# Routed two-layer network on one core: blocks of 512 rows with seven products, convolution in channel units over whole sequences

## The chip, the cores and the metric

The kernel runs on one NeuronCore of a Trainium2 chip. Its engines work side by side, each through its own instructions in order: TensorE (PE, with its weight loads as PEld), VectorE (DVE), ScalarE (ACT), GpSimd (POOL) and SyncE (SP), which here only issues transfers. The metric is the device time of one execution in microseconds (us). Before the change the median of three runs is 1327.32 us (1325.98 to 1328.85).

## The reference

The input is 8 sequences of 3584 tokens with 192 channels. First a causal convolution of 7 taps runs along each sequence; its taps are a softmax of `weight`, one set for each of 8 heads of 24 channels. Then each token is sent to one of 8 experts:

```python
out = np.einsum('hk,bskhg->bshg', w, x_unf)            # the convolution
logits = np.einsum('bsd,de->bse', x, w_gate)
local_gate = 1.0 / (1.0 + np.exp(-np.einsum('bsd,de->bse', x, w_local).squeeze(-1)))
e = fresh_e if s == 0 or local_gate[b, s] < 0.5 else prev_e
h = np.maximum(x[b, s] @ w1[e], 0.0)                   # 192 -> 1024
out[b, s] = p[e] * (h @ w2[e])                         # 1024 -> 192
```

A token whose local gate is at least one half keeps the expert of the token before it, so the choice runs along the sequence. `p` is the softmax of the logits. All values are 32-bit floats.

## The kernel before

**Groups and units.** The 28672 tokens are cut into 16 groups of 1792 (`PT`), two to a sequence. A unit is 128 rows of one expert (`UT`). Once a group is routed, its rows are scattered into a table in DRAM (`slots`), where each expert has its own stretch; units are read back from there.

**Groups 0 and 1** go a short way of their own at the start: `wide` (L195) does the convolution and the logits with TensorE, `wide_route` (L393) the routing. **Groups 2 to 15** are convolved by `conv` (L366): for each head ACT multiplies by the first tap (L377, 128x336) and DVE adds six more taps (L387). `route` (L601) then makes logits (`logits`, L565: DVE transposes into `z`, TensorE multiplies at L580, ACT copies to `ls`), carries the choice along the sequence with scans, and appends the rows to `to_put`. `table` (L788) writes which expert and which row of `slots` each coming block has.

**Blocks.** A block is one or two units of one expert (`n` = 1 or 2; `KT` = 2 is the most). The list (L885) has 35 blocks of one unit, then 87 of two, then 20 of one; two more single units stand behind a branch at the end (`spare`, L1108 and L1155) that is taken only when the table has something for them. How many blocks are surely full after each group is worked out ahead by `_sure` (L48) from the worst case, so the list does not depend on the data; which expert a block has is read from the table when it runs.

**One block** is: `load_w` (L897), 1536 KB of the expert's weights into one of four buffers `wb`; `load_rows` (L907), its rows into one of six buffers `xg`; `turn` (L928), transposes on TensorE into PSUM (`xps`) and four ACT copies to `xT`; `hidden` (L952), the first layer, 24 matmuls of 64 rows of the array times 128 columns for `n` = 2, in two PSUM pairs, each ended by two ReLU evictions on ACT (L968); `output` (L973), the second layer, 32 matmuls for `n` = 2, ended for each unit by an ACT eviction with scale (L988), a DVE addition (L992) and an indirect DMA of POOL that scatters the rows to the output (L996). A matmul uses half of the array's rows (`halves`), two run at once, and the profile has two records for each.

**The order of work** is written out by hand. In the loop over blocks (L1138) come the rows three blocks ahead (`ensure`, L1090), the weights three blocks ahead (`weights`, L1101), `hidden` of this block, `turn` of the next, `output` of this one. At three places of each block `step(time)` (L1037) inserts convolution or routing work for DVE until the given budget is used up; each piece of that work carries its own cost as a number (`yield 0.6`). `put` (L768) inserts one scatter of 128 rows into `slots` on POOL, behind a given instruction. Since every engine takes its instructions in order, this order decides what waits behind what. SP issues rows and then weights, and a load of convolution input from within `conv` (L385).

Of the kernel before, what the change touches and what calls it, by code (L numbers as in the profile page):

```python
# [9 lines left out]
I32 = mybir.dt.int32  # L10
# [23 lines left out]
NX = NT + HALO  # L34
# [4 lines left out]
KT = BT // P  # L39
# [4 lines left out]
EARLY = 3  # L44
SPARE = 2

# [5 lines left out]


ONE = [_sure(min(g + 1, EARLY) * PT, UT) for g in range(NPART)]
TWO = [_sure((g + 1) * PT - ONE[-1] * UT, BT) if g >= EARLY else 0 for g in range(NPART)]
# [3 lines left out]
FULL = {0: ONE[0], HALF: _sure(PT + PT // 2, UT), **{g: ONE[g] for g in range(1, NPART)}}  # L59
REST = NU - ONE[-1] - 2 * TWO[-1]  # L60
# [21 lines left out]
def kernel(  # L82
# [13 lines left out]
    xs = ctx.enter_context(tc.tile_pool(name="xs", bufs=2))  # L96
    ys = ctx.enter_context(tc.tile_pool(name="ys", bufs=4))
# [3 lines left out]
    xp = ctx.enter_context(tc.tile_pool(name="xp", bufs=6))  # L101
    tp = ctx.enter_context(tc.tile_pool(name="tp", bufs=1))
    hp = ctx.enter_context(tc.tile_pool(name="hp", bufs=1))
    op = ctx.enter_context(tc.tile_pool(name="op", bufs=2))
    xps_p = ctx.enter_context(tc.tile_pool(name="xps_p", bufs=1, space=PSUM))
    hps_p = ctx.enter_context(tc.tile_pool(name="hps_p", bufs=4, space=PSUM))
    yps_p = ctx.enter_context(tc.tile_pool(name="yps_p", bufs=2, space=PSUM))
# [6 lines left out]
    def load_x(g):  # L114
        x_sb = xs.tile([P, NX, D], F32, name="x_sb")
        src = x[g // PER]
        win = bass.AP(tensor=src.tensor, offset=src.offset + g % PER * PT * D,
                      ap=[[NT * D, P], [1, NX * D]])
        nc.sync.dma_start(out=x_sb.rearrange("p t d -> p (t d)"), in_=win)
        return x_sb  # L120

    def load_b(g):

        x_sb = xs.tile([P, NX, D], F32, name="x_sb")
        xv = x_sb.rearrange("p t d -> p (t d)")[:, :NB * D].rearrange("p (b d) -> p b d", d=D)
# [12 lines left out]
    with tc.tile_pool(name="scr", bufs=1) as scr:  # L138
# [4 lines left out]
        x_in = {0: load_b(0)}  # L143
        wg = cst.tile([P, 3 + DQ, Q], F32, name="wg")
        nc.sync.dma_start(out=wg, in_=wgl)
        x_in[1] = load_b(1)
# [43 lines left out]
    def z_tile():  # L190
        return yt.tile([P, 3 * NH * TB + NB * DR], F32, name="z")
# [3 lines left out]
    def wide(g, xv, y_sb, both):  # L195
# [58 lines left out]
        yr = zy[:TB, 3 * NH * TB:].rearrange("p (b d) -> p b d", d=DR)  # L254
# [17 lines left out]
        lt = sm.tile([P, NB, E + 1], F32, name="lt")[:TB]  # L272
# [9 lines left out]
    pi = cst.tile([P, 2], I32, name="pi")  # L282
    nc.gpsimd.iota(pi, pattern=[[0, 2]], base=0, channel_multiplier=1)
    ti0 = cst.tile([P, NT], I32, name="ti0")
# [78 lines left out]
    def row_tile():  # L363
        return ys.tile([P, NB, DG], F32, name="y_sb")
# [869 lines left out]
```

## Time and profile before

| what | value |
|---|---|
| median of three runs | 1327.32 us |
| the profiled execution | 1326.81 us |
| its span, first to last instruction | 1325.1 us |
| PE busy | 1304.4 us (98%) |
| DVE, ACT, POOL busy | 778.3, 625.2, 480.4 us |
| mean granted TensorE clock | 0.998 |
| moved by DMA | 325.29 MB, mean 245 GB/s |

The span is cut into 40 slices of 33 us in the page's second part, and each digit there is a busy share in tenths. A line of a group gives the source line, engine, operation, tiles written and read, shapes and count; then the busy time of the group and the mean duration of one in nanoseconds; then the idle time of the engine just before them and what ended it. In the timeline a line gives start and length of a run of like instructions and their count. PE's records overlap, so their starts tell more than their lengths.

### The profile page before, as it was taken

How to read it: one execution, taken by the hardware profiler on the slowest of the kernel's cores; microseconds unless marked ns; L12 is line 12 of the kernel's file. 1: busy time of each engine (PE TensorE's matmuls, PEld its weight loads, DVE VectorE, ACT ScalarE, POOL GpSimd, SP SyncE). 2: the span in 40 equal slices, each digit the busy share in tenths (PEclk: the TensorE clock that was granted, in tenths of full speed). 3: DMA queues.
4: the chain of work that ended last, by engine and by line, in shares of the span. 5: the costliest groups of instructions: out<-in, count | busy, mean ns of one | idle time of the engine just before them, and what ended most of it. 6: DMA issues, size and time to landing. Idle time of an engine off the chain costs nothing. (4 is left out here: it accounts for less than half of the span.)

```text
span 1325.1 us, 41356 instructions
## 1 busy us (share of the span) xinstructions
PE 1304.4 (98%) x16682; PEld 1260.9 (95%) x16682; DVE 778.3 (59%) x2434; ACT 625.2 (47%) x1571; POOL 480.4 (36%) x520
## 2 busy tenths in 40 slices
PE   9899999999999999999999999999999999999997
PEld 7799999999999999999999999999999999999997
DVE  6888898977878787878777878785610000000000
ACT  5345555544454545444545454544444444444553
POOL 4445352534343434343434343434344212211111
PEclk9999999999999999999999999999999999999999
DMA  5789999967575757575757575756565555556893
GB/s 188 283 349 391 376 365 345 394 213 266 182 275 177 290 188 277 201 260 192 271 186 273 193 271 199 267 195 210 197 211 205 189 185 188 192 187 229 313 317 131
DMA packets 67298, 325.29 MB, mean 245 GB/s; under 512 B 12576, under 2 KB 38103, under 8 KB 47650
## 3 DMA queue, kind: packets, MB, share of 16 engines
q1 hardware_dynamic: 44784, 277.41, 58.4%
q0 software_dynamic: 22320, 45.22, 9.2%
q8 instruction: 133, 2.18, 0.7%
q14 instruction: 59, 0.48, 0.1%
q10 hardware_dynamic: 2, 0.00, 0.0%
HBM read 277.29 MB, written 45.77 MB: 244 GB/s over the span
## 5 line engine op out<-in xcount | busy, mean ns | idle before, releaser
L980 PE MATMUL yps<-wb,hT 64*128 64x192 f32 x7328 | 641.0, 325 | 5.8 <-ACT hT L968 2.8
L963 PE MATMUL hps<-xT,wb 64*128 64x256 f32 (+1 forms) x6816 | 637.2, 336 | 1.7 <-issue 1.4
L963 PEld LDWEIGHTS hps<-xT,wb 64*128 64x128 f32 x6816 | 589.1, 187 | 27.2 <-issue 4.0
L980 PEld LDWEIGHTS yps<-wb,hT 64*128 64x128 f32 x7328 | 602.8, 187 | 11.1 <-issue 4.6
L996 POOL DMA_INDIRECT out_dram<-o_sb,xg x229 | 232.3, 1014 | 605.7 <-DVE o_sb L992 533.9
L968 ACT ACTIVATE hT<-hps 128x512 f32<-128x512 f32 (+1 forms) x568 | 261.9, 512 | 361.4 <-PE hps L963 246.5
L387 DVE SCALAR_TENSOR_TENSOR y_sb<-x_sb,c,y_sb 128x336 f32<-128x336 f32 x672 | 376.5, 570 | 18.9 <-issue 0.8
L992 DVE SCALAR_TENSOR_TENSOR o_sb<-yps,xg,o_sb 128x192 f32<-128x192 f32 x229 | 87.5, 414 | 467.8 <-ACT o_sb L988 461.4
L775 POOL DMA_INDIRECT slots<-y_sb,posi x228 | 231.2, 1014 | 209.3 <-ACT xT L949 114.8
L988 ACT ACTIVATE o_sb<-yps,xg 128x192 f32<-128x192 f32 x229 | 86.9, 418 | 289.8 <-PE yps L980 287.4
L949 ACT COPY xT<-xps 64x256 f32<-64x256 f32 (+4 forms) x568 | 210.8, 371 | 11.7 <-issue 1.7
L377 ACT ACTIVATE y_sb<-x_sb,c 128x336 f32<-128x336 f32 x112 | 63.7, 581 | 0.0
L359 PEld LDWEIGHTS xps<-ident,xg 64*128 64x128 f32 (+1 forms) x916 | 57.0, 124 | 5.2
L359 PE MATMUL xps<-ident,xg 64*128 64x64 f32 (+1 forms) x916 | 60.0, 217 | 0.0
L570 DVE STREAM_TRANSPOSE z<-y_sb 128x768 f32<-128x768 f32 (+1 forms) x56 | 45.4, 853 | 0.4
L596 DVE COPY lt<-lq 32x36 f32<-32x36 f32 x224 | 40.8, 182 | 3.5
L580 PE MATMUL hps<-z,wg 64*32 64x128 f32 x1344 | 24.2, 272 | 1.2 <-issue 1.2
L580 PEld LDWEIGHTS hps<-z,wg 64*32 64x32 f32 x1344 | 19.2, 105 | 4.1 <-issue 2.9
L556 PE MATMUL yps<-y_sb,hot 112*128 112x194 f32 x64 | 12.6, 353 | 1.4 <-DVE hot L550 1.1
L556 PEld LDWEIGHTS yps<-y_sb,hot 112*128 112x128 f32 x64 | 11.3, 202 | 2.1 <-DVE hot L550 1.6
L672 DVE COPY bk<-so_far 1x32 f32<-1x32 f32 x56 | 12.3, 220 | 0.7
L588 DVE STREAM_TRANSPOSE lq<-ls 128x256 f32<-128x256 f32 x14 | 6.2, 441 | 10.9 <-ACT ls L585 10.9
(236 smaller groups left out, 358.0 us busy)
## 6 DMA issues: line engine op xcount, KB each, us to landing
wb<-in_w_dram SPq DMA_DIRECT2D x138, 1536.0 KB
x_sb<-in_x_dram SPq DMA_DIRECT2D x14, 1920.0 KB
xg<-slots SPq DMA_DIRECT2D x87, 195.0 KB
wb<-in_w_dram SPq DMA_DIRECT2D x12, 512.0 KB
xg<-slots SPq DMA_DIRECT2D x53, 97.5 KB
out_dram<-o_sb,xg POOLq DMA_INDIRECT x229
slots<-y_sb,posi POOLq DMA_INDIRECT x228
x_sb<-in_xb_dram SPq DMA_DIRECT2D x4, 768.0 KB
```

Source lines behind the costliest of these rows:

```text
L359: nc.tensor.transpose(to, src[rows], identity=ident[rows, rows])
L377: nc.scalar.activation(cols(h), chans(h, 0), Act.Copy, scale=c[:, h, 0:1])
L387: nc.vector.scalar_tensor_tensor(cols(h), chans(h, k), c[:, h, k:k + 1], cols(h), Alu.mult, Alu.add)
L570: nc.vector.transpose(z[:, t:u, :], y_sb[:, t:u, Y0:Y0 + D])
L775: ins = nc.gpsimd.indirect_dma_start(out=slots[:, :], in_=rows, in_offset=None, out_offset=bass.IndirectOffsetOnAxis(ap=to, axis=0)).ins
L949: copied = nc.scalar.copy(a, b)
L963: nc.tensor.matmul(hps[half][:, j, w], lhsT=wb[rows, f0:f0 + P], rhs=xT[rows, d, w], start=(d == 0 and j == 0), stop=(d == KD - 1), skip_g ...
L968: relu = nc.scalar.activation(hT[:, m:m + 2, w], hps[half][:, :, w], Act.Relu)
L980: nc.tensor.matmul(yps[half][:, k * D:(k + 1) * D], lhsT=hT[rows, m, k * P:(k + 1) * P], rhs=wb[rows, WA + m * D:WA + (m + 1) * D], start= ...
L988: nc.scalar.activation(o_sb[:, k, :], y[k][0], Act.Copy, scale=xg[:, k, 0:1])
L992: nc.vector.scalar_tensor_tensor(o_sb[:, k, :], y[k][1], xg[:, k, 0:1], o_sb[:, k, :], Alu.mult, Alu.add)
L996: sent = nc.gpsimd.indirect_dma_start(out=out, in_=o_sb[:, k, :], in_offset=None, out_offset=bass.IndirectOffsetOnAxis(ap=xg.bitcast(I32)[ ...
```

## The change

- **Blocks of four units.** `KT` is now 4. The list becomes 51 blocks of one unit, 20 of two, 31 of four, none of a further kind of two, and 14 of one; behind the branch stand 28 single units, the first two in one branch and the rest in a second one inside it. Besides `_sure` there is `_likely`, which counts blocks as full that the worst case would not fill; `LOSE` units are held in reserve for it. The last single units form a group of their own (`PADS`), which waits for the filler rows; the others no longer do.
- **Seven products.** For a block of four units, the first layer's 192 input channels are three depths of 64 in each half of the array. For the first two depths, two row halves (256 rows) and two column halves of the weights are a 2x2 by 2x2 product of pieces, done with seven products in place of eight (`seven`), with sums of rows (`combine_x`, five DVE operations) and of weights (`combine_w`, four POOL operations on 256 columns, one in place). The third depth keeps four products. Partial sums are kept by ACT copies and joined by three DVE additions; ReLU follows. `output` then runs in two parts.
- **PSUM.** After the start, four pools of one pair of banks each (`xps_p`, `wps_p`, `yps_p`, `zps_p`) serve all uses.
- **Convolution.** The input is laid out by head. A unit of work is one head (24 channels) of one group (groups 2 and 3) or of a double group of 3584 rows, a whole sequence (the other twelve groups as six). `tap` starts a unit, `taps` may start some ahead. `route`, `logits` and their tiles take 28 rows per partition for a double group. The logits' matmuls are placed by `visit` in the middle of a later block's output or by the next step, in two halves.
- **Order.** SP issues tokens (`tokens`, at most two units of input per block), then weights, then rows. `step` carries an overshoot over to the next one; the budgets change.

The core of the diff:

```diff
-    xs = ctx.enter_context(tc.tile_pool(name="xs", bufs=2))
-    ys = ctx.enter_context(tc.tile_pool(name="ys", bufs=4))
+    xs = ctx.enter_context(tc.tile_pool(name="xs", bufs=1))
+    ys = ctx.enter_context(tc.tile_pool(name="ys", bufs=3))
...
+ONE = {g: _sure((g + 1) * PT, UT) if g + 1 < EARLY else _likely(EARLY * PT, UT, LEFT1) for g in GROUPS}
...
+blocks += [(2, 4, i, next(g for g in GROUPS if i < FOUR[g])) for i in range(FOUR[LAST])]
+blocks += [(3, 2, i, LAST) for i in range(PAIRS)]
+blocks += [(4, 1, i, PADS) for i in range(REST)]
...
+    def tokens():
+        for _ in range(2):
+            u = len(x_in)
+            if u == len(UNITS):
+                break
+            depth = 6 if UNITS[u][0] < EARLY else max(3, 21 - u) if u < 19 else 4
+            if u - depth > st["fin"]:
+                break
+            load_x(u)
...
+    def conv(u):
+        g, h = UNITS[u]
+        n = NT if g < EARLY else NS
+        tap(u)
+        yield 0
+        cols = got[g][:, :, Y0 + h * GS:Y0 + (h + 1) * GS]
+        for k in range(1, KC):
+            nc.vector.scalar_tensor_tensor(cols, x_in[u][:, k:k + n, :],
+                                           c[:, h, k:k + 1], cols, Alu.mult, Alu.add)
+            yield 0.6 if n == NT else 1.0
...
+    def combine_w(wb):
+        wt = hp.tile([P, 3, 2 * P], F32, name="wt")
+        b11, b12, b21, b22 = [wb[:, k * 2 * P:(k + 1) * 2 * P] for k in range(4)]
+        nc.gpsimd.tensor_tensor(wt[:, 1, :], b22, b12, op=Alu.subtract)
+        yield
+        nc.gpsimd.tensor_tensor(b12, b12, b11, op=Alu.subtract)
+        yield
+        nc.gpsimd.tensor_tensor(wt[:, 0, :], b22, b12, op=Alu.subtract)
+        yield
+        nc.gpsimd.tensor_tensor(wt[:, 2, :], b21, wt[:, 0, :], op=Alu.subtract)
+        yield wt
...
+    def combine_x(xT):
+        xc = hp.tile([P, 4, HU * P], F32, name="xc")
+        one, two = slice(0, HU * P), slice(HU * P, KT * P)
+        nc.vector.tensor_tensor(xc[:, 0, :], xT[:, 0, one], xT[:, 0, two], op=Alu.subtract)
+        nc.vector.tensor_tensor(xT[:, 0, two], xT[:, 0, two], xT[:, 1, two], op=Alu.add)
+        nc.vector.tensor_tensor(xc[:, 1, :], xT[:, 0, two], xT[:, 0, one], op=Alu.subtract)
+        nc.vector.tensor_tensor(xc[:, 2, :], xT[:, 1, one], xc[:, 1, :], op=Alu.subtract)
+        nc.vector.tensor_tensor(xc[:, 3, :], xT[:, 2, one], xT[:, 2, two], op=Alu.subtract)
+        return xc
...
+        times(xb, a11, b11, True)
+        nc.scalar.copy(h11, xb)
+        times(yb, s1, t1, True)
+        times(yb, a23, b32)
+        nc.scalar.copy(h22, yb)
+        times(xb, s2, t2)
+        nc.scalar.copy(h12, xb)
+        put(times(wbk, a12, b21, True))
+        times(wbk, a13, b31)
+        step(SIDE[0], None, 1)
+        nc.vector.tensor_tensor(h11, wbk, h11, op=Alu.add)
+        nc.scalar.activation(h11, h11, Act.Relu)
+        put(times(xb, s3, t3))
+        nc.vector.tensor_tensor(h22, xb, h22, op=Alu.add)
+        nc.scalar.activation(h22, h22, Act.Relu)
+        times(yb, s4, b22)
+        put(times(yb, s5, b32))
+        at = turn_next()
+        times(xb, a22, t4)
+        wt = weights_next()
+        next(wt)
+        put(times(xb, a23, b31))
+        next(wt)
+        nc.vector.tensor_tensor(h12, yb, h12, op=Alu.add)
+        nc.scalar.activation(h12, h12, Act.Relu)
+        nc.scalar.activation(h21, xb, Act.Relu)
...
+    def visit(bank):
+        if st["due"] and st["since"] < st["block"]:
+            st["bank"], st["due"], st["half"] = bank, False, True
+            route_op()
...
+            if spot and part == 0:
+                taps(min(n, 2), 3 - min(n, 2))
+            step((1.3 if n > 1 or st["block"] else 0) if n < KT else SIDE[2 + part])
...
+    SIDE = (2.4, 4.4, 1.6, 1.4)
...
     for i, (_, n, _, _) in enumerate(blocks):
         st["block"] = i
+        st["fin"] = st["unit"] - (st["cgen"] is not None)
+        tokens()
+        weights(i + AHEAD)
         ensure(i)
-        weights(i + AHEAD)
-        if i == LATE:
-            x_in[3] = load_x(3)
-        hT = hidden(n, wbs[i], xT, (1, 1) if i else (0, 0))
...
+        step(0.6 if i == 0 else 1.0 if n < n_next == KT else {1: 2.3, 2: 4.7, 4: SIDE[1]}[n])
+        output(n, wbs.pop(i), xgs.pop(i), hT, rows_next, between,
+               i != 1 and not n < n_next == KT)
+        if i == 1:
+            xT, _ = turn_in(n_next, turn_next())
...
+        if n < KT:
+            step(1.4 if n == 1 or n_next == KT else 3.6)
```

## The prediction

> **What bounds the kernel now.** I read the page's shares first, then its slices, then the groups by shape, then single blocks in the timeline, then stretches of the span.
>
> ```profile
> PE 1304.4 (98%) x16682; PEld 1260.9 (95%) x16682; DVE 778.3 (59%) x2434; ACT 625.2 (47%) x1571; POOL 480.4 (36%) x520
> DMA  5789999967575757575757575756565555556893
> ```
>
> TensorE is busy from end to end; the DMA engines are full only in slices 3 to 7, where single-unit blocks run. The groups by shape give the prices:
>
> ```profile
> L980 PE MATMUL yps<-wb,hT 64*128 64x192 f32 x7328 | 641.0, 325 | 5.8 <-ACT hT L968 2.8 <-DVE o_sb L992 1.9 <-issue 0.9
> L963 PE MATMUL hps<-xT,wb 64*128 64x256 f32 x4176 | 472.5, 376 | 0.0
> L387 DVE SCALAR_TENSOR_TENSOR y_sb<-x_sb,c,y_sb 128x336 f32<-128x336 f32 x672 | 376.5, 570 | 18.9 <-issue 0.8
> L968 ACT ACTIVATE hT<-hps 128x512 f32<-128x512 f32 x348 | 189.5, 595 | 288.9 <-PE hps L963 204.2 <-PE xps L359 78.9 <-issue 5.8
> L992 DVE SCALAR_TENSOR_TENSOR o_sb<-yps,xg,o_sb 128x192 f32<-128x192 f32 x229 | 87.5, 414 | 467.8 <-ACT o_sb L988 461.4 <-DMA xg<-slots 5.0 <-PE hps L963 0.9
> ```
>
> Everybody waits for PE; PE waits for others about 20 us in all. One quiet two-unit block in the timeline:
>
> ```profile
> 1049.04 5.34 PE L963 MATMUL hps<-xT,wb 64*128 64x256 f32 x48
> 1049.27 0.33 SPq L904 DMA_DIRECT2D wb<-in_w_dram  x1
> 1054.22 0.39 PE L359 MATMUL xps<-ident,xg 64*128 64x64 f32 x8
> 1054.45 5.42 PE L980 MATMUL yps<-wb,hT 64*128 64x192 f32 x64
> 1059.71 1.46 PE L963 MATMUL hps<-xT,wb 64*128 64x256 f32 x12
> 1059.94 0.33 SPq L904 DMA_DIRECT2D wb<-in_w_dram  x1
> ```
>
> From start to start: 48 records of the hidden product take 5.18 us (0.108 each), 8 transposes 0.23, 64 output records 5.26; the weights of the next block are issued every 10.67 us. At the end of the kernel single-unit blocks follow each other in 5.45 us:
>
> ```profile
> 1231.44 0.33 SPq L904 DMA_DIRECT2D wb<-in_w_dram  x1
> 1236.89 0.33 SPq L904 DMA_DIRECT2D wb<-in_w_dram  x1
> ```
>
> So a unit of 128 rows costs 5.45 us alone and 5.33 us in a pair: PE's time goes with the columns streamed, not with the blocks. The stretches (us, busy time of PE, PEld, DVE, ACT, POOL, clock, DMA share, GB/s) say how full the rest is:
>
> ```profile
> 100.00:160.00 60.00, 58.55 (x941) 57.02 (x940) 53.70 (x164) 32.47 (x101) 26.39 (x27) 1.00 0.99 390
> 1010.00:1110.00 100.00, 100.00 (x1132) 93.80 (x1132) 6.68 (x18) 42.85 (x96) 24.40 (x26) 1.00 0.57 198
> ```
>
> **The old time as a sum.** 55 single-unit and 87 two-unit blocks: 55 x 5.445 + 87 x 10.667 = 1227.5. The last matmul ends at 1318.3 and the first block would start at 49.3, so 41.5 us are extra: the 14 logits (weights' issues stretch by 1.7 to 2.1 us in the ten pair blocks, 3.0 to 3.3 in the four single ones: 31) and about 10 in other waits, nearly all before 258 us. After the last matmul 6.8 us follow. This execution took 1326.81 us, span 1325.1 and 1.7 around it; it is 0.5 below the median 1327.32.
>
> **The change, part by part.**
>
> *Units.* The formulas give 51 single, 20 pair and 31 four-unit blocks, then 14 single: 229 units as before (55 + 2 x 87). I counted the reference's own routing: every forecast of full blocks is met (53 singles where 51 are taken, exactly 31 fours at the end), the remainder is exactly 14 units, so the 28 spare blocks stay empty and their branch is not taken, as now. Ten units move from pairs to singles: 5 x (2 x 5.445 - 10.667) = **+1.1**.
>
> *Seven products.* A four-unit block makes 11 products of 8 records (7 + 4 in the third depth) where two pair blocks make 96 records: 88. All keep the 64x256 form, so 8 x 0.108 = 0.86 us each, x 31 = **-26.8**. Half a block change saved might add 1.5; I leave it out.
>
> *New additions and evictions in a four-unit block* (20.47 us of PE: 9.50 + 0.46 + 10.5). ACT: seven passes over 1024 elements (595 ns for 512 and 381 for 256 make 1.02 us), turned rows about 2.7, four outputs 1.7: 12 us. DVE: three additions of 1024 from PSUM. No such row exists; a DVE copy of 128x448 from PSUM (L236) takes 624 ns, 128x192 takes 414 (L992): extended by slope 1.25 to 1.3 us, in proportion to L992 2.2. I take 1.3, as 448 is nearest. With five subtractions of 256 (275 ns for 112 elements, so 0.43), four outputs and 9.8 budgeted steps DVE has 17 of 20.5 us. Now the path, from PE's start of a block with 0.863 per product: the tight place is bank pair xb, used by a22 x t4 at 8.23 us, behind h22's addition, behind h11's, which can start at 5.3: 5.3 + 2.6 = 7.9, so 0.3 us of slack. h12's copy ends at 4.8 (needed 5.18), h11's at 2.1 (needed 2.59). All covers hold, by tenths. Bounds: nothing, or the 1.5 us that 2.2 us per addition would cost; I take 0.06 per block, **+2**.
>
> *Weights combined on POOL*: four operations of 256. The nearest row is a POOL copy of 112x512 at 655 ns; bounds 0.3 to 1.3 us each. With ten scatters at 1.25 us pitch (those of the head start at 47.76, 49.01, 50.25) POOL has 14 to 18 of 20.5 us, and each product wanted is over 5 us away. Nothing; the cover is that distance.
>
> The Trainium skill (SBUF — State Buffer, "Who interferes with whom") speaks against it: a VectorE instruction with two SBUF inputs blocks against a GpSimd instruction reading SBUF. No row of this case shows such a pair side by side at length. By it, four times up to 0.7 us (an estimate from the rate in GPSIMD Engine Reference, "Elementwise — side-by-side cycle accounting") of DVE time could slip, 2.8 us of DVE's spare 3.5; where all fell ahead of h22 it would be 2.5 x 31 = 77 us, where none did, 0. The sum does without it.
>
> *Convolution in units of 24 channels, double groups of 3584 rows.* 96 instructions of 336 elements and 288 of 672 instead of 672 of 336; 672 elements by slope (570 at 336, 414 at 192) is 0.93, budgeted 1.0. DVE's share in single blocks (53.7 of 60 now) stays near 90%: a single block's steps go from 4.6 plus overshoot to 5.0 with the overshoot carried. Nothing, while DVE stays under PE.
>
> *Transfers in the single-unit stage.* Now per block: weights 1536 KB, rows 97.5, out 96, x 1920 KB and 14 scatters of 97.5 KB per group of 9.5 blocks: 2.125 MB in 5.445 us, 390 GB/s, the row above. After: 48 + 26 budgeted microseconds per double group at 5.0 per block are 15 blocks; x 8 x 408 KB, 28 scatters: 2.18 MB, 400 GB/s. At a ceiling of 390 that is 0.14 us per block, for 51 blocks instead of 35. Bounds: -2 (weights no longer queue behind SP's waiting rows) and +12 (blocks 39 to 47 carry three scatters each and want 420 GB/s). SP's new order puts up to two x loads and their wait for the unit four back, 2 to 3 us after the last block, ahead of the weights; these are issued three blocks (16 us) early, and rows, which come last, are the ones that lose it. I take **+3**.
>
> The row shows 390 GB/s at a DMA share of 0.99. The Trainium skill (DMA: Bandwidth & Descriptors, "Where 436 GB/s comes from") puts HBM transfers at about 358. By that figure a block of 2.18 MB would take 6.1 us, and 51 of them 33 us more than 5.45 each; by the row, 7.
>
> *Logits.* PE did all matmuls behind DVE's transposes; now their place is mid-output of a later block, in two halves. Pure matmul time is 24.2 / 14 = 1.73 each: 31 becomes 25, **-6** (bounds -8 and 0).
>
> *Head and handovers.* Seven convolution instructions leave route 1's chain (4.5 us of DVE between 41.7 and 47.1), all of gather 1 comes ahead, block 1's rows are turned behind its output (1.2 us of copies exposed): 0, bounds -4 and +4. Pairs to fours (all four POOL operations and five DVE ones at once) and fours to singles: **+2**, bounds 0 and 5. Forced scatters: group 5's 28 rows leave at 3 a block, POOL then has 4 x 1.25 = 5.0 of 5.45 us, and end about block 48, where block 51's rows are asked for: 0, at most 5.
>
> Sum: 1326.8 + 1.1 - 26.8 + 2 + 3 - 6 + 2 = **1302**.
>
> **Rivals.**
> - *Evictions show a little in every four-unit block* (0.5 us: ACT's taps or DVE's convolution ahead of an addition): +15, **1317**. For: 0.3 us of slack with in-order queues. Against: convolution is over by about block 80.
> - *Transfers bound the 51 single blocks*: +12, **1314**. For: DMA share 0.99 now. Against: PE lost 1.5 of 60 us there.
> - *Slower: the addition chain sets the block.* PE waits at a22 x t4 from 1.47 us per addition; from 1.88 (0.8 us lost x 31) the whole gain is gone; at 2.2 it is 1.5 x 31 = 46, **1348**. For: L992's own rate. Against: L236's.
> - *It does not do what it says*: spare blocks run, at over 5.45 us a unit. The counted routing excludes it.
>
> **How the numbers follow.** Chances: forecast 0.66 (own range 1290 to 1313), small stalls 0.14, transfers 0.09, addition chain 0.10, spares 0.01. The range 1285 to 1322 leaves out the last two and a few hundredths below. A change under 0.2% (2.7 us) cannot be told from none: same 0.03, taken from the upper edge of the stalls; slower 0.11; faster 0.86.
>
> **What would show it.** Right: four-unit blocks every 20.4 to 20.6 us, ACT and DVE waiting for PE in them, weights issued every 5.45 to 5.7 us in the first 51 blocks, PE's idle time still about 20 us. Wrong: PE idle ahead of products with a DVE or ACT releaser, 31 times alike; a DVE addition over 1.5 us; weights landing late at DMA shares of 1.0; PE waiting for rows at blocks 51, 62 or 71.

## The result and the profile after

The changed kernel takes 1337.97 us (median of four runs, 1336.58 to 1338.78) where the kernel before takes 1326.65 us (1325.81 to 1328.85). The ratio is 1.0082, with a 95% interval of 1.0064 to 1.0099: slower by 0.8%, where 1.9% faster was forecast and 1285 to 1322 us was the range. The profiled execution took 1336.58 us, its span 1334.8.

The kernels were timed in six sittings, always with the kernel before beside them, and the kernel before took 1327 to 1332 us in three of them and 1315 to 1316 us in the other three, so ratios are given throughout and the sitting is named by the time of the kernel before.

The page of the changed kernel, busy time and share by engine, then two rows of 40 slices:

```profile
PE 1294.2 (97%) x16674; PEld 1238.1 (93%) x16674; DVE 827.1 (62%) x1891; ACT 690.2 (52%) x1402; POOL 618.5 (46%) x650
PEclk9999999999899999999999999999999999999999
DMA  5898999999866757866342442424335233233592
```

TensorE's busy time fell by 10 us while the span grew by 10: TensorE now stands still for 41 us where it stood still for 21. DVE, ACT and POOL all do more. The DMA engines are nearly full in slices 2 to 11 and mostly under half full from slice 20 on.

The reading that decides is by units of work. Both kernels do the same 229 units of 128 rows in the same sequence, so the start of the k-th unit's last output matmul can be compared between them. In us, from the profiled executions:

```
units done                to 1   1-9   9-39   39-51  51-91  91-215  215-229  tail
before                    54.5  50.1  176.9   66.7  218.5   675.3    76.1    7.1
after                     56.9  57.5  174.2   85.2  229.0   646.3    76.2    9.2
difference                +2.4  +7.4   -2.7  +18.5  +10.5   -29.0    +0.1   +2.1
```

Units 91 to 215 are the four-unit blocks, and they gained what was forecast. Nearly everything was lost before them, where blocks of one and two units run: 18.5 us in twelve single units, 10.5 us in twenty pair blocks, 7.4 us in units 2 to 9.

The four-unit blocks, in the timeline of SyncE in the changed kernel (start, length):

```profile
1025.32 0.33 SPq L1013 DMA_DIRECT2D wb<-in_w_dram  x1
1045.74 0.33 SPq L1013 DMA_DIRECT2D wb<-in_w_dram  x1
1066.16 0.33 SPq L1013 DMA_DIRECT2D wb<-in_w_dram  x1
```

and the three additions of one block in the timeline of VectorE:

```profile
1009.09 1.22 DVE L1147 TENSOR_TENSOR h<-ps,h 128x1024 f32<-128x1024 f32 x1 [3.74 <-PE ps L1132]
1010.23 1.22 DVE L1150 TENSOR_TENSOR h<-ps,h 128x1024 f32<-128x1024 f32 x1
1011.66 1.23 DVE L1160 TENSOR_TENSOR h<-ps,h 128x1024 f32<-128x1024 f32 x1 [0.22 <-PE ps L1132]
```

A block every 20.42 us (forecast 20.47), an addition in 1.22 us (forecast 1.3), and VectorE waits for TensorE's products, not the other way round.

Where the time went shows in the waits. SyncE's queue and TensorE in the changed kernel (total, times, longest):

```profile
SPq L1013 <- PE ps L1177: 676.0, 77, 21.6
SPq L157 <- DVE y_sb L467: 191.9, 41, 12.0
SPq L1020 <- DMA out_dram<-o_sb,xg: 81.9, 39, 5.7
```

```profile
PE ps L401 <- DMA xg<-slots: 10.2, 4, 4.9
PE ps L1080 <- issue: 5.9, 16, 0.9
PE ps L1177 <- issue: 4.1, 4, 3.0
```

L157 issues tokens, L1013 weights, L1020 rows, in this order in each block. The rows stand behind two waits that are not theirs: for a free buffer of tokens (192 us in all) and for a free buffer of weights (676 us). Then TensorE waits for rows: four times, 10.2 us; the kernel before has no such line. The second kind, "issue", is TensorE standing still while nothing that it needs is missing; it comes up again below. One of the four, the first block of a group whose rows have only just been scattered, in the timelines of SyncE and of TensorE:

```profile
475.62 11.00 SPq L1013 DMA_DIRECT2D wb<-in_w_dram  x2
487.38 2.27 SPq L1020 DMA_DIRECT2D xg<-slots  x3
```

```profile
486.07 5.35 PE L1080 MATMUL ps<-xT,wb 64*128 64x256 f32 x48
494.40 0.45 PE L401 MATMUL ps<-ident,xg 64*128 64x64 f32 x8 [2.98 <-DMA xg<-slots]
```

The two weight loads are 10.7 us apart, since the second waits for TensorE to leave its buffer; only 1.1 us after it come the rows, behind 1536 KB on the same queue, and TensorE waits for them.

### The profile page after: what moved, and what is told of

It reads as the page before. It is cut to its first block, busy times and chain, and to the rows that moved or that the text cites. A ratio compares the mean times of both kernels' runs of the same rounds, so it can differ in the third digit from the quotient of the medians.

```text
span 1334.8 us, 40951 instructions
## 1 busy us (share of the span) xinstructions
PE 1294.2 (97%) x16674; PEld 1238.1 (93%) x16674; DVE 827.1 (62%) x1891; ACT 690.2 (52%) x1402; POOL 618.5 (46%) x650
## 4 chain that ended last, share of the span: by engine, by line
PE 88%; DMA 3%; DVE 3%; issue 3%; ACT 1%; POOL 1%; another core or an unknown queue 0%; SPq 0%; POOLq 0%; DVEq 0%; ACTq 0%
PE ps L1177 44%; PE ps L1132 21%; PE ps L1080 19%; DMA xg<-slots 3%; PE ps L401 2%; PE ps L668 2%; DVE y_sb L467 1%; DMA slots<-y_sb,posi 1%; PE hps L250 1%; POOL slots L875 0%; DVE hot L630 0%; PE hps L195 0%; ACT xT L1058 0%; DVE o_sb L1193 0%
## 5 line engine op out<-in xcount | busy, mean ns | idle before, releaser
L1177 PE MATMUL ps<-wb,h 64*128 64x192 f32 x7328 | 635.6, 326 | 5.7 <-issue 4.1
L1177 PEld LDWEIGHTS ps<-wb,h 64*128 64x128 f32 x7328 | 604.5, 188 | 13.1 <-issue 10.8
L467 DVE SCALAR_TENSOR_TENSOR y_sb<-x_sb,c,y_sb 128x672 f32<-128x672 f32 (+1 forms) x384 | 322.4, 848 | 47.3 <-ACT y_sb L426 33.8
L1080 PE MATMUL ps<-xT,wb 64*128 64x128 f32 (+1 forms) x4080 | 304.2, 298 | 7.9 <-issue 5.9
L1080 PEld LDWEIGHTS ps<-xT,wb 64*128 64x128 f32 x4080 | 283.2, 188 | 22.5 <-issue 13.1
L1193 DVE SCALAR_TENSOR_TENSOR o_sb<-ps,xg,o_sb 128x192 f32<-128x192 f32 x229 | 87.8, 413 | 324.3 <-ACT o_sb L1187 296.2
L1187 ACT ACTIVATE o_sb<-ps,xg 128x192 f32<-128x192 f32 x229 | 87.5, 419 | 327.9 <-PE ps L1177 286.8
L1084 ACT ACTIVATE h<-ps 128x256 f32<-128x256 f32 (+1 forms) x340 | 128.9, 431 | 159.9 <-PE ps L1080 103.7
L1058 ACT COPY xT<-ps 128x128 f32<-128x128 f32 (+2 forms) x464 | 194.1, 418 | 15.8 <-PE ps L401 7.6
L1132 PE MATMUL ps<-xT,wb 64*128 64x256 f32 x1488 | 178.0, 376 | 0.6 <-DVE xT L1110 0.6
L1132 PEld LDWEIGHTS ps<-xT,wb 64*128 64x128 f32 x1488 | 151.4, 187 | 8.6 <-issue 1.0
L401 PE MATMUL ps<-ident,xg 64*64 64x64 f32 (+1 forms) x916 | 49.8, 219 | 10.2 <-DMA xg<-slots 10.2
```

Of the source, the lines that this page charges most:

```text
L401: nc.tensor.transpose(to, src[rows], identity=ident[rows, rows])
L467: nc.vector.scalar_tensor_tensor(cols, x_in[u][:, k:k + n, :], c[:, h, k:k + 1], cols, Alu.mult, Alu.add)
L1058: copied = nc.scalar.copy(a, b)
L1080: nc.tensor.matmul(hps[:, half, j, :], lhsT=wb[rows, f0:f0 + P], rhs=xT[rows, d, :], start=(d == 0 and j == 0), stop=(d == KD - 1), skip_g ...
L1084: relu = nc.scalar.activation(hT[two][:, half], hps[:, half], Act.Relu)
L1132: ins = nc.tensor.matmul(to[:, half, j, :], lhsT=b[rows, j * P:(j + 1) * P], rhs=a[rows, :], start=(first and j == 0), stop=True, skip_gro ...
```

## The experiments

The theory after the first reading (A): SyncE's order costs most of the loss. Rivals: the transfers' volume (the DMA engines are full in the single-unit blocks); the blocks of four units are not worth what the columns say; GpSimd's scatters, which are stretched and hold buffers.

**Twelve products in the four-unit blocks.** `seven` becomes twelve direct products, without sums.

```diff
-        t2, t3, t4 = [wt[:, k, :] for k in range(3)]
...
-        s3, s2, s4, s5 = [xc[:, k, :] for k in range(4)]
...
-        times(yb, s1, t1, True)
-        times(yb, a23, b32)
-        nc.scalar.copy(h22, yb)
...
+        times(xb, a12, b21)
+        times(xb, a13, b31)
+        nc.scalar.activation(h11, xb, Act.Relu)
...
```

> The four-unit blocks make the plain twelve products again: 96 records in place of 88, no additions, no combined weights or rows; the list of blocks, the convolution units and the order stay as changed. Theory (seven products give what was forecast, the loss lies elsewhere): a quiet four-unit block goes from 20.42 to 21.3 us, 31 of them cost 27 us, 1338 becomes 1363 to 1367. Rival (the seven products bring their own waits, so that they gain little or lose): within 8 us of 1338.

Measured 1360.17 us, ratio 1.0247 (1.0212 to 1.0282), 3 us below the range expected. Units 91 to 215 take 668.5 us for 646.3, 22.2 us more, and units 1 to 91 as long as the changed kernel's within 1 us. A quiet block now takes 21.29 us in SyncE's timeline, against 20.42:

```profile
1060.65 0.33 SPq L1013 DMA_DIRECT2D wb<-in_w_dram  x1
1081.94 0.33 SPq L1013 DMA_DIRECT2D wb<-in_w_dram  x1
```

So the products are worth 0.87 us in a quiet block, 27 us in 31 of them. The stage shows only 22.2, because the changed kernel has some 13 us beyond 31 quiet blocks there and this kernel 8 to 9. The gain of the change is real; the loss lies elsewhere.

**Rows, then weights, then tokens.** Only SyncE's order of issue is changed.

```diff
-        tokens()
-        weights(i + AHEAD)
         ensure(i)
+        weights(i + AHEAD)
+        tokens()
```

> SyncE issues rows, then weights, then tokens, all else as changed. Theory A (SyncE's order: the wait for a free input buffer stands ahead of weights and rows, 192 us of it in all): block 6's stall of 5.2 us and part of the late stalls go, 1338 becomes 1322 to 1331. Theory B (transfers saturated in the single-unit stage) and theory C (POOL's scatters slowed by DVE's longer instructions): within 4 us of 1338.

Measured 1327.67 us, ratio 0.9994 (0.9980 to 1.0008), beside 1328.17 us: the 0.8% is gone. The waits of SyncE, and TensorE no longer waits for rows:

```profile
SPq L1020 <- DMA out_dram<-o_sb,xg: 387.8, 85, 9.8
SPq L157 <- DVE y_sb L467: 19.8, 10, 3.6
```

The same block's rows are now issued as soon as they are there, ahead of the weights:

```profile
479.35 2.27 SPq L1020 DMA_DIRECT2D xg<-slots  x3
482.38 0.33 SPq L1013 DMA_DIRECT2D wb<-in_w_dram  x1
```

By units the gain is 4.8 us in units 2 to 9 (57.5 to 52.7) and 2.4 each in 39 to 51 (85.2 to 82.8) and 51 to 91 (229.0 to 226.6). But 25 us to the forecast remain.

**Half the weights.** Single-unit blocks from the fifth on load half of the weights' bytes, 768 KB each, and use that half for both layers, so the second layer's result is another.

```diff
-        step = WA + WB if i > AHEAD else (WA + WB) // 3
-        for x0 in range(0, WA + WB, step):
+        half = i > AHEAD and blocks[i][0] == 0
+        step = WA if half else WA + WB if i > AHEAD else (WA + WB) // 3
+        for x0 in range(0, WA if half else WA + WB, step):
```

> Blocks 4 to 50 load only the first half of their weights and use it for both layers, so the second layer's result is another; 768 KB less per block, 2.18 MB becomes 1.4. Theory B (transfers): the 34 us that the 50 single blocks lose beyond 5.445 each and the logits fall below 10, 1338 becomes 1308 to 1316. Theory C (POOL): the 16 us of blocks 39 to 50 stay, 1322 to 1330, and scatters there still take 1.3 to 1.6 us. Theory A (order): 1330 or more.

Measured 1332.24 us, ratio 1.0033 (1.0016 to 1.0051): with 37 MB less to move 0.5% is gained (1.0082 to 1.0033), some 6 us. Units 39 to 51 still take 84.5 us. The volume is not what bounds these blocks.

**What a scatter costs beside VectorE.** A kernel of its own: 20 scatters of 128 rows on GpSimd alone, then beside runs of three VectorE instructions.

> Not the computation: five stretches of 20 indirect scatters of 128 rows on POOL, the first with DVE idle, then beside additions of 672 elements with two SBUF inputs, of 336 elements with two, of 672 elements with one input, and of 672 with two again. Nothing else moves. Theory C: 0.95 to 1.0 us a scatter alone, 1.3 to 1.6 beside 672 elements with two inputs, 1.0 to 1.1 beside 336, under 1.05 beside one input. Theory B (the long scatters are the saturated transfers): 0.95 to 1.05 in all five.

One scatter of each stretch in the timeline of GpSimd (the third and fourth of each are alike), in the order alone, beside 672 elements with two inputs, beside 336 with two, beside 672 with one:

```profile
15.38 0.97 POOL L55 DMA_INDIRECT out_dram<-rows,at  x1 [0.30 <-issue]
42.01 1.60 POOL L55 DMA_INDIRECT out_dram<-rows,at  x1 [0.30 <-issue]
43.92 1.60 POOL L55 DMA_INDIRECT out_dram<-rows,at  x1 [0.30 <-issue]
84.31 0.97 POOL L55 DMA_INDIRECT out_dram<-rows,at  x1 [0.30 <-issue]
126.82 0.97 POOL L55 DMA_INDIRECT out_dram<-rows,at  x1 [0.31 <-issue]
```

Beside the convolution's new instruction a scatter takes 1.60 us for 0.97, and one comes every 1.91 us for every 1.28: just two of VectorE's instructions, which start every 0.95 us there (43 in 40.99). Size and inputs both matter: 336 elements with two inputs cost nearly nothing (two of twenty took 1.32), 672 with one cost nothing. In the changed kernel the scatters that lie beside such an instruction, 134 of them, average 1.31 us; in the kernel before those beside 336 elements average 1.06. The Trainium skill ("SBUF — State Buffer", section "Who interferes with whom") says that a VectorE instruction with two SBUF inputs contends with a GpSimd instruction that reads SBUF, but infers that the making of descriptors for a transfer is spared, as it needs the write side. The scatter reads its row numbers from an SBUF tile (`at`), and 1.60 us beside two inputs of 672 against 0.97 beside one agrees with the first statement; the 0.97 us beside two inputs of 336 shows that it does not hold at every size. Which part of the scatter waits no run shows, so the inference is neither confirmed nor refuted.

**Three repairs of the scatters**, each on top of rows, weights, tokens. First, two group scatters per single block in place of three:

```diff
-            if shares and (n == 2 or two or len(to_put) > (NT if st["block"] % 2 else 2 * NT)
-                           or to_put and to_put[0][0] >= EARLY):
+            if shares and (n == 2 or two or len(to_put) > (NT if st["block"] % 2 else 2 * NT)):
```

> Rows, weights, tokens as in the run before, and the clause that gives a scatter of rows a second place in the hidden product of single-unit blocks for the later groups is taken out: two group scatters per single block in place of three. What is left there after the order was undone is 17.5 us over twelve quiet blocks (39 to 50), 3.5 of them logits. Theory P (GpSimd's queue: four scatters of up to 1.9 us pitch in a block of 5.45 us, stretched by the convolution's 672-element instructions, so that an output scatter lands late and holds its output and row buffers): three at 1.9 fit nearly, 1319 to 1324 us, but the 28 rows of the group of blocks 51 on are then forced out at block 49 and may give 3 to 5 us back. Theory Q (what is left there is TensorE's own: instruction supply and transfers, whatever GpSimd does): 1326 to 1329, no change.

Second, more buffers for the single-unit blocks, cut from tiles that only the four-unit blocks use:

```diff
+        if blocks[i][0] == 0 and i % 2:
+            at = i // 2 % 5 * DG
+            xg = rings[0][:, at:at + DG].rearrange("p (k d) -> p k d", k=1)
+        else:
+            xg = xp.tile([P, KT, DG], F32, name="xg")
...
+            if st["block"] < ONE[LAST]:
+                to = st["block"] % 5 * D
+                o_sb = rings[1][:, to:to + D].rearrange("p (k d) -> p k d", k=1)
```

> The order rows, weights, tokens, and in the single-unit blocks five more row buffers and five output buffers for two, in memory that only the four-unit blocks use. Theory P: a late output scatter no longer holds the next rows or the next eviction; the waits of SyncE for output scatters (388 us in all) nearly vanish in the first 51 blocks and the time falls to 1314 to 1322 us, though GpSimd stays as full. Theory Q: 1326 to 1329, no change.

Third, the convolution's instructions cut in two while scatters are waiting:

```diff
+            cuts = 2 if n == NS and to_put else 1
+            m = n // cuts
+            for r in range(0, n, m):
+                nc.vector.scalar_tensor_tensor(cols[:, r:r + m], x_in[u][:, k + r:k + r + m, :],
+                                               c[:, h, k:k + 1], cols[:, r:r + m], Alu.mult, Alu.add)
```

> The order rows, weights, tokens, and every convolution instruction of 672 elements that is issued while group scatters are waiting is cut in two of 336. Theory P: scatters beside the convolution fall from 1.31 to 1.0 us, GpSimd has 4 x 1.3 = 5.2 of 5.45 us, and blocks 39 to 50 lose less; VectorE pays 0.2 us per instruction (2 x 0.57 against 0.94), 1 us in a block that already has 5.1 of 5.45 us on it, so 1318 to 1328 us. Theory Q: scatters fall the same way and the time doesn't, 1326 to 1335.

And buffers and cut together:

> More buffers and the cut convolution together. Theory P: if the buffers cover what a late scatter holds, the cut adds nothing to them: within 3 us of the buffers alone; if GpSimd's own rate is the limit, 3 to 8 us below the buffers alone. Theory Q: 1326 to 1335.

Measured, beside 1316.27 us of the kernel before: two scatters 1302.44 us, ratio 0.9891 (0.9874 to 0.9907); more buffers 1295.37 us, 0.9837 (0.9821 to 0.9854); cut 1305.66 us, 0.9916 (0.9896 to 0.9936); buffers and cut 1298.70 us, 0.9871 (0.9854 to 0.9887). All four lie far below what was expected, but the kernel before is 12 us faster too: this is a different sitting, and the times expected from the first one cannot be read against it. Among themselves the four can be compared: buffers alone are the fastest, and the cut on top of them costs 3.3 us. The next comparison has the order alone beside the changed kernel in such a sitting.

The cut shows one thing without a comparison. Scatters beside it did not fall to 1.0 us: they average 1.52 us, and 22 of all scatters take 2 to 10.5. GpSimd and VectorE in the timeline of this kernel:

```profile
281.17 3.99 POOL L878 DMA_INDIRECT slots<-y_sb,posi  x1 [0.30 <-ACT h L1087]
284.57 4.86 DVE L470 SCALAR_TENSOR_TENSOR y_sb<-x_sb,c,y_sb 128x336 f32<-128x336 f32 x10
285.47 4.81 POOL L878 DMA_INDIRECT slots<-y_sb,posi  x1 [0.30 <-ACT h L1087]
289.70 4.87 DVE L470 SCALAR_TENSOR_TENSOR y_sb<-x_sb,c,y_sb 128x336 f32<-128x336 f32 x10
290.58 0.99 POOL L878 DMA_INDIRECT slots<-y_sb,posi  x1 [0.30 <-DMA slots<-y_sb,posi]
291.88 1.16 POOL L1201 DMA_INDIRECT out_dram<-o_sb,xg  x1 [0.30 <-DVE y_sb L470]
```

Ten halves take 4.86 us, about 0.49 each, closer together than in the measurement above, where 336 elements took 0.58 each and a scatter was hardly held. The scatter that starts among them at 285.47 lasts until 290.28, past the end of all ten. That a scatter waits wherever such instructions follow each other without a gap would fit this, but not the next two: at 290.58 and 291.88 they take 0.99 and 1.16 us beside ten more halves at the same pace. What decides whether a scatter is held by such a run stays open.

**The changed kernel, the order, old order with buffers, and both repairs, side by side.**

> The changed kernel as it is, beside the kernel before on one chip with the three runs below. In the last runs the kernel before took 1316.3 us, on the first chip 1326.7: TensorE's stretches without a wait (10 us in single-unit blocks of the change on the first chip) had nearly gone. Theory C (the first chip's slow supply is part of the 0.8% loss, more of it in the change, which keeps its buffers and queues fuller): where before takes 1316 the change takes 1302 to 1312, a ratio of 0.990 to 0.997; where before takes 1326, 1.006 to 1.010. Theory O (the order and the scatters alone, whatever chip): 1.006 to 1.010 on both.

> Rows, weights, tokens once more, in the same comparison. Both theories: 8 to 12 us below the changed kernel beside it if the order's cost is the chip's own business nowhere; theory C with a fast chip: 2 to 8 us below, because rows that are issued late still land in time there.

> The changed kernel's order (tokens, weights, rows) with five more row buffers and five output buffers for two in the single-unit blocks. If SyncE's wait for a free token buffer is what costs, buffers for rows don't help it: within 4 us of the changed kernel, and 8 us or more above the buffers with rows first (ratio 0.984 to the kernel before). If held row and output buffers are what costs, whatever the order: the same 0.984, and 12 to 20 us below the changed kernel.

> Rows first, more buffers and two group scatters per single block in place of three: whether the two repairs add. If both relieve the same held buffers: within 3 us of the buffers alone (0.981 to 0.986 of the kernel before). If GpSimd's own rate still costs beside them: 4 to 8 us less (0.978 to 0.981).

The kernel before took 1314.85 us. The changed kernel 1310.02 us, ratio 0.9964 (0.9951 to 0.9978): here it is faster, by 0.4%. The order alone 1300.65, 0.9892 (0.9878 to 0.9906), 9.4 us below the changed kernel: in the range (8 to 12) for a cost that does not depend on the sitting, not in the 2 to 8 that theory C gave. Old order with more buffers 1311.74, 0.9977 (0.9967 to 0.9986): buffers do not help while the rows stand at the end of the queue. Rows first, buffers and two scatters 1300.47, 0.9890 (0.9876 to 0.9905): no better than the order alone, and the two-scatter repair takes back what buffers give (units 39 to 51 take 75.5 us with it and 70.7 without; TensorE waits 3.5 us for rows once, which I put down to the rows left over being forced out together).

The rest of theory C holds: part of the loss belongs to the sitting, and it hits the change harder. Theory O falls. What the waits show in this sitting, first ScalarE and TensorE of the changed kernel:

```profile
ACT o_sb L1187 <- DMA out_dram<-o_sb,xg: 10.1, 4, 4.1
```

```profile
PE ps L401 <- DMA xg<-slots: 12.1, 6, 3.9
PE ps L1080 <- issue: 0.8, 2, 0.6
```

then ScalarE and TensorE with rows first:

```profile
ACT o_sb L1187 <- DMA out_dram<-o_sb,xg: 7.6, 2, 6.1
```

```profile
PE ps L401 <- DMA xg<-slots: 1.7, 1, 1.7
```

Rows first takes TensorE's wait for rows from 12.1 to 1.7 us; ScalarE's evictions still wait for a late output scatter that holds one of two output buffers. In the first 348 us, where the single-unit blocks lie, SyncE waits for late output scatters as well, before it can issue rows:

```profile
SPq L1020 <- DMA out_dram<-o_sb,xg: 147.9, 37, 8.8
```

With more buffers ScalarE has no such wait, and SyncE's comes to 0.4 and 7.1 us in the sittings at 1316 and 1315 us.

**Which part of the order, and what the sitting moves.** Four more, with the kernel before as a run of its own for its profile:

> The kernel before, with its own profile. Theory C (stretches without a wait, in which TensorE, GpSimd and SyncE get no instructions to run, are a matter of the sitting): where it takes about 1315 us its 11.5 us of TensorE gaps without a wait fall to 5 or less, the head shortens by 2 to 5 us, and its blocks are the same 5.445 and 10.667 us; where it takes 1327 the profile is the old one. If the gaps are unchanged at 1315 us, theory C falls and something else in the blocks moved.

> Rows first and more buffers, beside rows first alone in the same comparison. In the profiles the twelve blocks 39 to 50 lose 5.4 us beside 10.2 with the order alone: if the buffers do that, 3 to 7 us below the order alone; if the difference was one between sittings, within 2 us.

> Rows, weights, tokens: 0.989 of the kernel before where that takes about 1315 us, 0.999 where it takes 1327.

The last one issues weights, rows, tokens:

```diff
+        weights(i + AHEAD)
         ensure(i)
-        weights(i + AHEAD)
         tokens()
```

> Weights, rows, tokens. If the tokens' wait for a free input buffer is what holds the queue (192 us of waiting in the changed kernel, 20 to 25 with tokens last): within 2 us of rows, weights, tokens. If the rows' place behind the weights matters as well (1536 KB ahead of 97.5 KB on the same queue): 4 to 8 us slower than that.

The kernel before took 1331.77 us. Rows, weights, tokens: 1330.45, ratio 0.9993 (0.9982 to 1.0004). Weights, rows, tokens: 1338.94, 1.0057 (1.0044 to 1.0069). The 8.5 us between them are the rows' place behind the weights; the tokens, which wait last in that kernel, add little to it: 0.25% by the ratios (1.0082 with tokens first, 1.0057 with weights first, in different sittings), some 3 us. I had taken their wait for the main thing. TensorE waits for rows again:

```profile
PE ps L401 <- DMA xg<-slots: 6.3, 3, 3.1
```

More buffers 1332.44, 1.0005 (0.9995 to 1.0015): no gain at all here, beside the order alone in the same sitting, where 3 to 7 us had been expected if the buffers are what helps. SyncE's wait for late output scatters in the single-unit blocks falls here too, from 153.8 to 8.3 us; the time does not follow. The kernel before, profiled: span 1334.1.

**The last pair**, which fell into a sitting with the kernel before at 1315.18 us:

> Theory C: where it takes about 1315 us, TensorE's gaps of over 0.1 us without a wait, 10 us at 1327 and 17 us at 1331, are 5 us or less (5.3 to 6.5 in the changed kernel's variants in such sittings), and the head is 2 to 7 us shorter; where it takes 1326 or more they are 10 to 20 us again. If they are 10 us or more at 1315, the gaps are not what moves the time.

> Rows first and more buffers: 0.982 to 0.986 of the kernel before where that takes about 1315 us, if its gain is one of the fast sittings (the late output scatters are then the last thing in the way); 0.998 to 1.002 where it takes 1326 or more, where gaps without a wait take the gain.

Rows first with more buffers took 1295.31 us, ratio 0.9858 (0.9841 to 0.9876), 1.4% faster than the kernel before, 0.34% better than the order alone in the other sitting of this kind. It beats both kernels there; in the sitting of 1332 us it equals the kernel before.

One thing that differs between the sittings is how long TensorE stands still with nothing to wait for. Summed over each trace, gaps of more than 0.1 us ahead of a matmul that waits for no semaphore:

```
kernel                       kernel before takes 1327 to 1332   takes 1315 to 1316
before                              10.0, 17.4 us                    4.9 us
after                               17.5                             6.5
rows, weights, tokens               20.8, 16.7                       5.3
the same, more buffers              24.4                             5.4, 4.3
half the weights                    16.0                             -
```

In the view of waits of the kernel before at 1315 us the lines that end in "issue" are:

```profile
PE yps L980 <- issue: 1.6, 2, 1.1
PE hps L963 <- issue: 0.6, 1, 0.6
```

The gaps are about half of what separates the sittings: 5.1 us of 10.3 between two traces of the kernel before (10.0 and 4.9 us, spans 1325.1 and 1314.8), 11.0 of 20.3 between two of the changed kernel (17.5 and 6.5, spans 1334.8 and 1314.5). What the other half is stays open. The mean granted clock is not it: 0.998 and 0.997 in the kernel before, 0.992 and 0.993 in the changed one.

The changed kernel pays most in the twelve units 39 to 51, where single-unit blocks and forced scatters meet. In the sittings at 1327 to 1332 us they take 85.2 us as changed, 82.8 with rows first and 83.9 with more buffers; at 1315 us they take 77.2, 75.6 and 70.7. The kernel before takes 66.7 and 65.9. So at 1327 us hardly any of the largest loss in the table, 18.5 us, goes with these repairs. TensorE's waits in these units and the stretch itself (us; PE, PEld, DVE, ACT, POOL busy; granted clock; DMA share; GB/s) in the changed kernel, then the stretch with rows first at 1315 us:

```profile
PE ps L1080 <- issue: 5.1, 13, 0.9
PE ps L401 <- DMA xg<-slots: 1.6, 1, 1.6
288.70:373.90 85.20, 77.83 (x1206) 72.12 (x1206) 60.85 (x112) 39.33 (x118) 49.34 (x40) 0.96 0.91 332
272.40:347.90 75.50, 72.22 (x1206) 69.97 (x1204) 60.63 (x112) 38.66 (x118) 49.74 (x40) 0.98 0.93 349
```

A pause costs more than its own length where TensorE's granted clock falls to a half behind it. In stretches of the changed kernel (us; PE, PEld, DVE, ACT, POOL busy; granted clock; DMA share; GB/s), after TensorE's 4.9 us wait for rows at 91.7 us:

```profile
86.00:93.70 7.70, 5.71 (x88) 5.52 (x84) 6.11 (x12) 3.91 (x12) 4.30 (x5) 1.00 0.98 347
93.70:100.50 6.80, 3.86 (x26) 3.89 (x28) 1.61 (x4) 1.64 (x5) 1.33 (x2) 0.50 1.00 376
100.50:107.00 6.50, 6.50 (x102) 6.50 (x102) 5.28 (x9) 2.78 (x9) 2.48 (x3) 1.00 0.73 263
```

The cause of the gaps stays open. They are not the core's own volume of transfers: with half the weights there are 16.0 us of them. They lie no closer to the loads of instructions in the trace (16 KB each, one every 9 to 10 us) than chance would have it: 27% of them come within 3 us after one in the changed kernel, where 30% of the time lies. All traces in the table have 10 us and more in the sittings at 1327 to 1332 us and 4 to 7 in those at 1315 to 1316. What else was on the chip no trace shows. The Trainium skill ("HBM Reference", section "Specifications (TRN2)") says that two cores share the bandwidth of one memory domain; nothing here shows whether a neighbour was at work.

The units once more, in sittings at 1315 us (the profiled execution of the changed kernel was its slowest there, 1316.2 us):

```
units done                to 1   1-9   9-39   39-51  51-91  91-215  215-229  tail
before                    51.2  51.7  170.7   65.9  218.6   673.6    76.1    7.1
after                     52.4  55.3  174.2   77.2  226.3   643.8    76.1    9.2
rows, weights, tokens     50.0  49.5  172.8   75.6  222.1   643.3    76.1    9.4
the same, more buffers    49.3  49.4  172.3   70.7  222.1   643.3    76.1    9.0
```

## Why the prediction was wrong, step by step

- **Units and Seven products** were right. Single units take 5.445 us, pairs 10.667, four-unit blocks 20.42 (forecast 20.47). Units 91 to 215 gain 29.0 us where 26.8 less 2 were forecast. The run with twelve products has quiet blocks of 21.29 us: the products give 0.87 us per block where 0.86 was reckoned, and the longer block by itself gives 0.05 (two pair blocks take 21.33), which is the 1.5 us in 31 blocks that I had left out. The stage gains 29.0 also because two of the fourteen logits have moved out of it: six lie in these units before, four after.
- **New additions and evictions** were right in size, 1.22 us for an addition (forecast 1.25 to 1.3), and cost nothing in the quiet blocks; +2 was not needed there. The rival of an addition chain that sets the block is dead, and so is that of small stalls in every four-unit block.
- **Weights combined on POOL** were right: 764 ns for one on average, within the bounds of 0.3 to 1.3 us, and hidden. Scatters, which the step did not have in mind, are what a VectorE instruction with two inputs holds up in these runs (1.60 us for 0.97).
- **Transfers in the single-unit stage** is the step that failed most. It named the right thing, SyncE's new order, in which "rows, which come last, are the ones that lose it", and priced it within +3 (bounds -2 and +12) on the strength of loads that are issued three blocks early. That cover does not exist for the first blocks of a group: their rows are asked for only one or two blocks ahead, as soon as the group's scatters are out. Then 1536 KB of weights, and the wait of the weights for TensorE, stand in front. The order costs 8.5 us (weights against rows) to 11.7 us (0.88% of 1327, changed kernel against rows first). The volume, of which the step's sum was made, is worth some 6 us when half of the weights are left out, in a sitting at 1328 us. The 358 GB/s of the page named there did not bind: 388 GB/s in the changed kernel's stretch from 160 to 250 us.
- **Forced scatters** (0, at most 5) was mis-sized. Four scatters per block at 1.25 us made 5.0 of 5.45 us; they last 1.31 us beside the convolution and take 1.6 with the pause, so four of them, all beside it, would need 6.4 us, an estimate, and more than the block. The late output scatters hold their buffers: with more buffers units 39 to 51 take 70.7 us for 75.6, in two sittings at 1315 us, but 83.9 for 85.5 side by side at 1332 us, where the whole kernel gains nothing. The duration came from rows beside 336 elements, and the change that doubles the size of the convolution's instructions was in the same diff: this row was not one of the changed kernel's.
- **Logits** (-6) did not come. The sum took the matmuls' busy time, 1.73 us each, for what a block would lose. In the ten pair blocks before, one took 1.52 us from its first record to the next matmul and stretched the block by 1.7 to 2.1, so little could be saved there. Now a half takes 0.87 us, 1.74 for one of the fourteen, and two four-unit blocks that hold one each last 22.57 and 22.56 us in place of 20.42, 2.14 more. If all fourteen cost as much, that is 30 us, an estimate, where 31 were before. SyncE's weights in the kernel with rows first, in a sitting at 1315 us:

```profile
780.92 0.33 SPq L1013 DMA_DIRECT2D wb<-in_w_dram  x1
...
803.49 0.33 SPq L1013 DMA_DIRECT2D wb<-in_w_dram  x1
...
826.05 0.33 SPq L1013 DMA_DIRECT2D wb<-in_w_dram  x1
```

  Why a half costs 0.2 us more than its matmuls was not tried.
- **Head and handovers** (0 and +2): the head came out 2.4 us longer to the first unit (1.2 at 1315 us), and the tail 2.1 us longer, which was not in the sum. What the handovers cost was not read apart.
- **What no step held**: the gaps without a wait. The kernel before had 10 us of them in the very trace that the forecast was made from ("about 10 in other waits"), and I took them as fixed. In a sitting with few of them the changed kernel takes 1310 us and the same with rows first 1301, against a sum of 1302 that started from 1326.8.

So against the forecast's gain of 24.8 us, in a sitting with few gaps 4.8 were there. Of the 20 missing, 9.4 are the order, by two runs side by side. The held buffers are 4 to 7, by ratios from different sittings (0.9892 without them, 0.9858 and 0.9837 with them). The last 4 to 6 no run took apart; the logits that were not saved are as much. In the recorded comparison another 16 us are the sitting's: the changed kernel loses 28 us between the two kinds of sitting (1338.0 to 1310.0), the kernel before 11.8 (1326.65 to 1314.85). Half of that 16 is in units 39 to 51 (85.2 and 77.2 us, against 66.7 and 65.9). Why the change loses more there is open: that its busier queues and fewer buffers leave less to ride over a pause with is only argued, and more buffers did not help at 1332 us.

The rival that transfers bound the single-unit blocks (1314) was nearest by place, and its mechanism was wrong as well. No rival ended slower through SyncE's order, although the order stood in the change's own words.

## What to carry to other kernels

When an in-order queue gets a new order, price it by the transfer that is asked for latest, not by those that are asked for early: here a small load that was sometimes urgent belonged ahead of a large one that was issued three blocks early. When two parts of a change meet on one engine, take the duration of the meeting instruction under the new neighbour; here a scatter's 1.06 us beside the convolution turned into 1.31 on average when the neighbour had doubled. And time a change of one or two per cent in more than one sitting: here the sign depended on it.

## What was not expected of the hardware

- A scatter of 128 rows on GpSimd took 0.97 us alone, 1.60 beside VectorE instructions of 672 elements with two SBUF inputs, 0.97 beside 672 with one input and, but for two of twenty, beside 336 with two. With the convolution cut in halves, 22 scatters took 2 to 10.5 us, and others beside the same halves 1.0.
- The same kernel took 1315 or 1327 to 1332 us, the runs of one kernel in one sitting within about 0.6% of each other; in it and its successors TensorE paused 4 to 7 or 10 to 24 us for no reason that the trace shows.
- With a pause of 4.9 us the granted clock was 0.50 for 6.8 us, from within the pause on; 3.9 us of that were work at half speed, so the pause cost some 1.9 us more.
